# State products of a pair placed behind the outputs of the pair in front, in the unused half of their bank

## The chip, the cores and the metric

The kernel runs on one core of a Trainium2 chip. The core has TensorE (matrix products into PSUM), VectorE (DVE in the profile), ScalarE (ACT), GpSimd (POOL), SyncE (SP, which issues transfers) and 16 DMA engines. The metric is the time of one execution on the device in microseconds (us); lower is better. Numbers like L519 are lines of the kernel's source. The changed kernel has its own line numbers.

## The reference

Two blocks follow each other. The first is a state space recurrence over 4 batches of 8 heads with 768 time steps each, head size 32 and state size 16:

```python
log_a = np.log(np.clip(a, 1e-06, 1.0))
for c in range(nc):                       # chunks of 32 steps
    cum = np.cumsum(la, axis=-1)
    L = np.exp(cum[..., :, None] - cum[..., None, :]) * causal
    CB = np.einsum('bhin,bhjn->bhij', Cc, Bc)
    y_intra = np.einsum('bhij,bhjd->bhid', CB * L, xc)
    y_inter = np.einsum('bhin,bhnd->bhid', Cc, state) * np.exp(cum)[:, :, :, None]
    y[:, :, sl] = y_intra + y_inter
    Bx = np.einsum('bhjn,bhjd->bhjnd', Bc, xc) * decay_from_j[..., None, None]
    state = decay_full[:, :, None, None] * state + np.sum(Bx, axis=2)
```

Its outputs, as 3072 tokens of 256 features, go through a two-layer block with a leaky slope per hidden feature (2048 hidden features):

```python
h = x @ w_in
g = np.maximum(h, 0.0) + alpha * np.minimum(h, 0.0)
return g @ w_out
```

All is in float32.

## The kernel before

The kernel takes chunks of 128 steps and handles them in pairs: 12 pairs, 0 to 11, three to a batch. Two pairs make a group of 512 tokens; there are 6 groups. For each pair TensorE transposes B and C, multiplies them ("gram" products), adds up the outputs y, and makes the state products (B, scaled by the decays to the end of the chunk, times x). For the last pair of a batch only the first chunk's state is needed. The second block runs per group in four "quads" (z = 0 to 3), each with seven products in and seven products out: a two-by-two matrix product done with seven instead of eight products. While group g goes through its quads, the two pairs of group g + 1 are worked in between, piece by piece. Group 0 has been through the second block in another, simpler way before that.

A pair is a generator: each `next` runs it up to its next `yield`. `fine` is true for pairs 4 to 11.

```python
def pair(gp):
    ...
    tp = spare() if gp == 1 else ss_tile()
    for i in range(2):
        for k in range(2):
            nc.tensor.transpose(tp[:, (2 * i + k) * P : (2 * i + k + 1) * P], nat[:, i, k], ident)   # L469
    bc = work.tile([P, 4, Q], F32, name="bc")
    nc.scalar.copy(out=bc.rearrange("p i t -> p (i t)"), in_=tp)
    ...
    bn = bns.pop(gp) if gp in bns else pair_loads(gp)      # GpSimd: B times the decays (L385)
    ...
    def added(dps):                                        # the state products
        dps = dps.rearrange("p (k m) -> p k m", m=P)
        for k in range(nk):                                # nk = 1 for the last pair of a batch, else 2
            for w in range(KC):
                ws = slice(64 * w, 64 * w + 64)
                nc.tensor.matmul(dps[ws, k], bn[:, k, ws], xt[:, k, w * P : (w + 1) * P],     # L519
                                 start=True, stop=True, tile_position=(0, 64 * w), ...)
        return dps

    def states(dps):                                       # VectorE adds the decayed old state
        ...                                                # (ScalarE copies, for a batch's first)
        nc.gpsimd.tensor_tensor(out=sm[:, :nk], in0=new[:, :nk], in1=hmask..., op=ALU.mult)   # L534

    if fine:
        for k in range(2):
            for w in range(2):
                half_decays(k, w)                          # two scans on VectorE each (L438)
                if k == 1 and w == 1:
                    spread_c()
                yield
    ...
        if fine:
            states(added(ss_tile()))
            c_decayed()                                    # GpSimd
        yield
        gram = products_bc()
    ... # gram times decays on VectorE, with a yield in the middle and one behind
    y = [ss_tile()[:, : 2 * Q].rearrange("p (k t) -> p k t", k=2) for w in range(KC)]
    ... # 4 products with the states (L620) and 16 with dec and x (L627) into y[0] and y[1]
    for w in range(KC):
        nc.scalar.copy(out=xts[g][:, w, q * Q : (q + 2) * Q], in_=y[w]...)                    # L634
```

`ss_tile` gives a PSUM tile of 128 x 512 numbers, which is a whole bank; two banks take turns. A y fills half of its bank.

The quad, cut to its order. `first` puts two products of the first layer into half-filled tiles A or Y; `after(j)` is where products of the second layer, steps of the pairs and other work come in:

```python
first(A, b11); copy m1 <- A (ScalarE); after(1)
first(Y, t1);  copy m5 <- Y (ScalarE); after(2); after(3)
first(A, t2);  copy u2 <- A (ScalarE, L787); after(4)
Y = Y + u2 (VectorE, L789); after(5)
first(A, t3);  c22 = A + m5 (VectorE, L793); after(6)
first(Y, b22); prelu of Y and c22 (ScalarE L753, VectorE L755); copy Y <- m1 (ScalarE, L799)
after(7); after(8)
first(A, t4);  prelu of A; after(9); after(10)
first(Y, b21); prelu of Y; ... after(11) to after(14)
```

The steps of the pairs in the quads, with `nxt` the first pair of the group ahead:

```python
token_sums(1)
ssm(2 * GC // 2, 2)                 # pair 4, two steps: transposes, first scans
steps = {(0, 1): 0, (0, 2): 0, (0, 5): 0, (0, 9): 0, (0, 13): 0, (1, 1): 0, (1, 5): 0,
         (1, 12): 1, (1, 14): 1, (2, 1): 1, (2, 2): 1, (2, 5): 1, (2, 9): 1, (2, 13): 1,
         (3, 1): 1, (3, 5): 1, (3, 12): 2, (3, 14): 2}
...
def after(j, ...):
    places = with_gram if nxt < NP and z % 2 == 0 else without
    if i and j in places:
        product(*divmod(NZ + i - 1, NZ), places[j])        # second-layer products, L745
    ...
    if nxt + steps.get((z, j), NP) < NP:
        ssm(nxt + steps[z, j])
    if nxt < NP and (z, j) == (3, 7):
        token_sums(g + 1)                                  # GpSimd, L725
    ahead = nxt + {(1, 3): 1, (3, 8): 2}.get((z, j), NP)
    if ahead < NP:
        ...
        bns[ahead] = pair_loads(ahead)                     # bn of the pair ahead
```

Of the kernel before, what the change touches and what calls it, by code (L numbers as in the profile page):

```python
# [9 lines left out]
F32 = mybir.dt.float32  # L10
U32 = mybir.dt.uint32
U16 = mybir.dt.uint16
ALU = mybir.AluOpType
# [9 lines left out]
def kernel(  # L23
# [25 lines left out]
    nc = tc.nc  # L49
# [6 lines left out]
    P = 128  # L56
    Q = 128
# [6 lines left out]
    KC = d_model // P  # L64
    NF = d_ff // P
    GC = 4
    GT = GC * Q
    NG = NCH // GC
    NP = NCH // 2
# [18 lines left out]
    work = ctx.enter_context(tc.tile_pool(name="work", bufs=2))  # L88
# [4 lines left out]
    gp = ctx.enter_context(tc.tile_pool(name="gp", bufs=16))  # L93
    op = ctx.enter_context(tc.tile_pool(name="op", bufs=3))
# [172 lines left out]
    def keep_warm(to, n, cols=2 * Q):  # L267

        for i in range(n):
# [8 lines left out]
                          in_=ident.unsqueeze(1).to_broadcast([P, H, Q]))  # L278
# [11 lines left out]
    hmask = bmask[:, :P]  # L290
# [30 lines left out]
    state = {}  # L321

    masked = {}
# [2 lines left out]
    held = {}  # L326
    bns = {}

    def identity_bank():
# [47 lines left out]
    def pair_loads(gp):  # L377

        b, c = divmod(2 * gp, CPB)
        nat, abc, xt, ap = loads["p", gp]  # L380

        bn = work.tile([P, 2, H * N], F32, name="bn")
        i, bi = divmod(b, 2)
        pj = prt[i].rearrange("p (b h c) -> p b c h", b=2, h=H)[:, bi, c : c + 2]
        nc.gpsimd.tensor_tensor(  # L385
            out=bn.rearrange("p k (h n) -> p k h n", h=H),
            in0=nat[:, 0].rearrange("p k (h n) -> p k h n", h=H),
            in1=pj.unsqueeze(3).to_broadcast([P, 2, H, N]), op=ALU.mult)
        return bn
# [22 lines left out]
    def spare():  # L412

        return ps_h.tile([P, GT], F32, name="hp", tag="hp")

    def pair(gp):

        b, c = divmod(2 * gp, CPB)
        nat, abc, xt, ap = loads["p", gp]
        last = c + 2 == CPB  # L420
        dec = work.tile([P, 2, H, Q], F32, name="dec")
        dv = dec.rearrange("p k h t -> p k (h t)")

# [18 lines left out]
        ahead = {}  # L442

        pf = ap
        if gp == 0:
            z = first_a(ap, nc.vector)
# [5 lines left out]
                                    op1=ALU.min)  # L452
# [8 lines left out]
            yield  # L461


        tp = spare() if gp == 1 else ss_tile()
        if gp == 0:
            keep_warm(tp, 3, Q)
# [22 lines left out]

        fine = gp >= 2 * GC // 2  # L490
        if gp < 2:
            spread_c()
        if gp == 0:
# [1 line left out]
            dps = spare()  # L495
            keep_warm(dps, 6, Q)
            yield
        bn = bns.pop(gp) if gp in bns else pair_loads(gp)
        if gp == 1:
            c_decayed()  # L500
            dps = spare()
# [1 line left out]
        elif gp:  # L503
            yield

        nk = 1 if last else 2
        st = [masked.get(b)]  # L510
        new = work.tile([P, 2, P], F32, name="state")
        sm = work.tile([P, 2, P], F32, name="sm")

        def added(dps):
            dps = dps.rearrange("p (k m) -> p k m", m=P)
            for k in range(nk):
                for w in range(KC):
                    ws = slice(64 * w, 64 * w + 64)
                    nc.tensor.matmul(dps[ws, k], bn[:, k, ws], xt[:, k, w * P : (w + 1) * P],  # L519
                                     start=True, stop=True, tile_position=(0, 64 * w),  # L520
                                     skip_group_check=True)
            return dps

        def states(dps):
            for k in range(nk):
                old = state.get(b)
                if old is None:
                    nc.scalar.copy(out=new[:, k], in_=dps[:, k])
                else:
                    e = (k + 1) * Q - 1  # L530
                    nc.vector.scalar_tensor_tensor(out=new[:, k], in0=old, scalar=pf[:, e : e + 1],
                                                   in1=dps[:, k], op0=ALU.mult, op1=ALU.add)
                state[b] = new[:, k]
            nc.gpsimd.tensor_tensor(out=sm[:, :nk], in0=new[:, :nk],  # L534
                                    in1=hmask.unsqueeze(1).to_broadcast([P, nk, P]), op=ALU.mult)
            st.extend(sm[:, k] for k in range(nk))
            masked[b] = st[-1]

        if fine:
            for k in range(2):  # L540
                for w in range(2):
                    half_decays(k, w)
                    if k == 1 and w == 1:
                        spread_c()
                    yield
        else:
            if gp > 1:
                states(added(ss_tile()))
                c_decayed()
# [33 lines left out]
        if gp == 0:  # L583
            gram = products_bc()
            dps = added(dps)
            yield
            c_decayed()
            times(dec[:, :, :2], one_less(gram))
        elif gp == 1:
            decays(1)  # L590
            gram = products_bc()
            g0 = one_less(gram)
            states(dps)
            times(dec[:, :, :2], g0)
        else:
            if fine:
                states(added(ss_tile()))
                c_decayed()
            yield
            gram = products_bc()  # L600
        for i, r in enumerate(r for r in ((2, 3, 0, 1) if fine else (3, 2, 1, 0) if gp > 1 else range(4))
                              if r in gram):
# [6 lines left out]
        yield  # L609


        y = [ss_tile()[:, : 2 * Q].rearrange("p (k t) -> p k t", k=2) for w in range(KC)]
        if gp < 2:
            keep_warm(y[0].rearrange("p k t -> p (k t)"), 2 - gp)
        begun = False
# [359 lines left out]
    for f in range(FIRST, NF):  # L975
# [21 lines left out]
        if f in in_steps:  # L997
            weight_sums(wi, in_sums, 0, in_steps[f])
    early[0] = None
    token_sums(1)  # L1000
    ssm(2 * GC // 2, 2)


    steps = {(0, 1): 0, (0, 2): 0, (0, 5): 0, (0, 9): 0, (0, 13): 0, (1, 1): 0, (1, 5): 0,
             (1, 12): 1, (1, 14): 1, (2, 1): 1, (2, 2): 1, (2, 5): 1, (2, 9): 1, (2, 13): 1,
             (3, 1): 1, (3, 5): 1, (3, 12): 2, (3, 14): 2}

    late_sums = {(0, 2): ((wqt, out_sums, 0, 0),), (0, 4): ((wqt, out_sums, 0, 1),),
# [11 lines left out]
    for i in range(NZ * (NG - 1)):  # L1020
        g, z = divmod(NZ + i, NZ)
        nxt = 2 * g + 2

        def after(j, g=g, z=z, i=i, nxt=nxt):
            places = with_gram if nxt < NP and z % 2 == 0 else without
            if i and j in places:
                product(*divmod(NZ + i - 1, NZ), places[j])
            if i == 0:
                for f, half in last_out.get(j, ()):
                    output(NF - LATE + f, half)  # L1030
            if (i, j) in ((0, 13), (1, 8)):
# [24 lines left out]
        quad(g, z, after)  # L1056
# [31 lines left out]
```

## Time and profile before

| | before |
|---|---|
| time, median of 3 | 376.63 us (376.53 to 378.01) |
| span of the profiled execution | 375.5 us |
| TensorE busy, products | 365.0 us, 97% |
| VectorE / ScalarE / GpSimd busy | 242.4 / 179.1 / 202.1 us |
| state products L519, all pairs | 80 records, 7.0 us (5.7 into ss, 1.3 into hp) |

A busy time counts an engine's instructions, not its waits. A float32 product is recorded as two passes, each with its own weight load (PEld), so two chunks of state products, 4 instructions, appear as x8. In a line of a timeline the columns are start, length, engine, source line, operation, output <- input, shapes, how many, and in brackets how long the engine sat idle ahead of it and which instruction ended that. Runs of like instructions are merged. "issue" means that the profile shows nothing the engine waited for.

### The profile page before, as it was taken

The numbers are of one execution on the slowest core, as the hardware profiler recorded it, in microseconds if no ns is written. First come the engines' busy times: TensorE is split into PE (matmuls) and PEld (weight loads), VectorE is DVE, ScalarE is ACT, GpSimd is POOL, SyncE is SP. The second block draws the span as 40 slices with busy tenths as digits, with TensorE's granted clock in tenths as the row PEclk, the third lists the DMA queues.
The fourth block names the chain that finished last, engine by engine and source line by source line (L and its number), as shares of the span: only waits on it lengthen the run. The fifth ranks groups of instructions, "written<-read, shape, count | busy, mean of one in ns | idle before, by whom it ended". The sixth has DMA issues, their size and how long they took to land.

```text
span 375.5 us, 6180 instructions
## 1 busy us (share of the span) xinstructions
PE 365.0 (97%) x2223; PEld 294.9 (79%) x2223; DVE 242.4 (65%) x461; ACT 179.1 (48%) x384; POOL 202.1 (54%) x212
## 2 busy tenths in 40 slices
PE   8899899899999999999999999999999999999996
PEld 8676566468878788788788788788788788888884
DVE  7997959967537737747737847637847734544364
ACT  1557757425354445445445535535625525553541
POOL 4875665468856835535555445456354355264512
PEclk9999999999999999999999999999999999999999
DMA  7999898551008801002802801901811001001003
GB/s 141 222 178 290 238 234 207 146 104 58 28 19 160 159 3 56 2 0 45 165 4 47 164 2 34 178 0 23 152 38 26 5 0 20 11 0 30 1 0 84
DMA packets 121878, 30.71 MB, mean 82 GB/s; under 512 B 93736, under 2 KB 117752, under 8 KB 121848
## 3 DMA queue, kind: packets, MB, share of 16 engines
q1 hardware_dynamic: 116736, 29.74, 35.9%
q10 hardware_dynamic: 5112, 0.59, 1.1%
q8 instruction: 17, 0.28, 0.3%
q14 instruction: 13, 0.11, 0.1%
HBM read 26.98 MB, written 3.34 MB: 81 GB/s over the span
## 4 chain that ended last, share of the span: by engine, by line
PE 86%; DVE 6%; POOL 2%; ACT 2%; issue 1%; POOLq 0%; DVEq 0%; ACTq 0%
PE hp L770 33%; PE bank L745 32%; PE bank L684 4%; PE hp L646 3%; DVE dec L438 2%; PE ss L627 2%; PE hp L661 2%; PE ss L569 2%; PE ss L620 1%; PE ss L469 1%; PE ss L519 1%; PE hp L569 1%; PE hp L270 1%; DVE gt L650 1%; DVE wr L239 1%
## 5 line engine op out<-in xcount | busy, mean ns | idle before, releaser
L813 POOL TENSOR_TENSOR gt<-gt 128x512 f32<-128x512 f32 x58 | 73.6, 1269 | 31.4 <-DVE gt L755 24.5
L755 DVE SCALAR_TENSOR_TENSOR gt<-hp,s_mul,gt 128x256 f32<-128x256 f32 x120 | 52.5, 479 | 47.7 <-ACT gt L753 46.4
L745 PE MATMUL bank<-gt,w_out 128*128 128x256 f32 x320 | 82.5, 382 | 0.4 <-ACT o_sb L691 0.4
L753 ACT ACTIVATE gt<-hp,s_alpha 128x256 f32<-128x256 f32 x120 | 50.3, 470 | 46.8 <-PE hp L770 32.7
L745 PEld LDWEIGHTS bank<-gt,w_out 128*128 128x128 f32 x320 | 60.0, 190 | 11.2 <-issue 2.3
L804 POOL TENSOR_TENSOR gt<-gt 128x512 f32<-128x512 f32 x20 | 25.4, 1270 | 77.7 <-DVE gt L755 77.7
L745 PE MATMUL bank<-gt,ws 128*128 128x256 f32 x240 | 58.3, 379 | 0.0
L745 PEld LDWEIGHTS bank<-gt,ws 128*128 128x128 f32 x240 | 45.1, 190 | 5.8
L438 DVE TENSOR_TENSOR_SCAN dec<-abc,bank 128x256 f32<-128x256 f32 x80 | 48.1, 661 | 0.0
L770 PE MATMUL hp<-xs,w_in 128*128 128x256 f32 x160 | 42.8, 390 | 0.0
L770 PE MATMUL hp<-xT,w_in 128*128 128x256 f32 x160 | 41.9, 384 | 0.0
L770 PE MATMUL hp<-xs,ws 128*128 128x256 f32 x160 | 41.1, 379 | 0.0
L789 DVE TENSOR_TENSOR hp<-hp,u 128x512 f32<-128x512 f32 x20 | 14.0, 700 | 39.6 <-ACT u L787 39.6
L778 ACT COPY m<-hp 128x512 f32<-128x512 f32 x20 | 11.7, 586 | 51.5 <-PE hp L770 51.5
L770 PEld LDWEIGHTS hp<-xs,w_in 128*128 128x128 f32 x160 | 28.7, 189 | 7.7 <-issue 3.3
L770 PEld LDWEIGHTS hp<-xT,w_in 128*128 128x128 f32 x160 | 29.7, 190 | 5.1 <-issue 1.2
L770 PEld LDWEIGHTS hp<-xs,ws 128*128 128x128 f32 x160 | 30.4, 190 | 4.1
L684 PEld LDWEIGHTS bank<-w_out,gt 128*128 128x128 f32 x128 | 24.2, 190 | 8.7 <-issue 5.8
L684 PE MATMUL bank<-w_out,gt 128*128 128x256 f32 x128 | 30.5, 380 | 0.0
L646 PE MATMUL hp<-xT,w_in 128*128 128x512 f32 x48 | 23.2, 605 | 3.4 <-DVE gt L650 2.6
L793 DVE TENSOR_TENSOR c<-hp,m 128x512 f32<-128x512 f32 x20 | 13.6, 681 | 19.3 <-PE hp L770 19.3
L787 ACT COPY u<-hp 128x512 f32<-128x512 f32 x20 | 11.7, 585 | 23.0 <-PE hp L770 23.0
(155 smaller groups left out, 554.0 us busy)
## 6 DMA issues: line engine op xcount, KB each, us to landing
abc<-z SPq DMA_DIRECT2D x20, 512.0 KB, 4.8
raw<-in_moe_w_in_dram SPq DMA_DIRECT2D x8, 512.0 KB, 4.9
raw<-in_moe_w_out_dram SPq DMA_DIRECT2D x8, 512.0 KB, 6.3
xt<-in_x_dram SPq DMA_DIRECT2D x24, 128.0 KB, 3.9
out_dram<-o_sb SPq DMA_DIRECT2D x32, 64.0 KB, 1.9
nat<-in_B_dram SPq DMA_DIRECT2D x22, 64.0 KB, 2.6
nat<-in_C_dram SPq DMA_DIRECT2D x22, 64.0 KB, 2.6
ap<-pf SPq DMA_DIRECT2D x11, 128.0 KB
```

What stands on the lines that cost most here:

```text
L438: nc.vector.tensor_tensor_scan(out=dv[:, k, hs], data0=abc[k][:, hs], data1=ident_p[0], initial=0.0, op0=ALU.mult, op1=ALU.add)
L646: nc.tensor.matmul(hp, w_in[:, k, f * P : (f + 1) * P], xts[g][:, k], start=(k == 0), stop=(k == KC - 1))
L684: nc.tensor.matmul(pos[0][t // 2][:, t % 2], gt[:, t * Q : (t + 1) * Q], w_out[:, f], start=(f == 0 and t % 2 == 0), stop=(f == NF - 1), s ...
L745: nc.tensor.matmul(ms[g][i][:, h], w, blocks[g, z][n][:, p], start=(q == 0 and h == 0), stop=(q == NQ - 1), skip_group_check=True)
L753: nc.scalar.mul(o[:, p], h[:, p], s_alpha[:, fs[p]])
L755: nc.vector.scalar_tensor_tensor(out=o[:, p], in0=h[:, p], scalar=s_mul[:, fs[p]], in1=o[:, p], op0=ALU.mult, op1=ALU.max)
L770: nc.tensor.matmul(to[:, p], w(2 * z + p), b, start=start and p == 0, stop=True, skip_group_check=True)
L778: nc.scalar.copy(out=m1, in_=A)
L789: nc.vector.tensor_tensor(out=Y, in0=Y, in1=u2, op=ALU.add)
L793: nc.vector.tensor_tensor(out=c22, in0=A, in1=m5, op=ALU.add)
L804: nc.gpsimd.tensor_tensor(out=tc_, in0=g22, in1=g12, op=ALU.subtract)
L813: eng.tensor_tensor(out=o, in0=x0, in1=x1, op=ALU.subtract)
```

## The change

The state products of a pair leave their own step in the even quads, (0, 9) and (2, 9). They come at (1, 5) and (3, 5), straight behind the outputs of the pair in front, and go into the second half of the bank that holds that pair's y[1]. That takes one PSUM tile per pair out of the rotation. On TensorE the products with small tiles (the outputs, 32 columns wide, and the state products, 64 wide) then stand side by side, and the stream of full products in the even quads is no longer broken at (z, 9). For this bn must be ready sooner, so GpSimd makes it at (0, 9) and (2, 9) instead of (1, 3) and (3, 8). `c_decayed` moves to the last scan. Pair 4, which has no fine pair in front, gets a tile of its own, and its state products become its first step, ahead of its transposes.

```diff
@@ pair
+        if fine:
+            bn = bns.pop(gp) if gp in bns else pair_loads(gp)
+            states(added(beside.pop(gp) if gp in beside else ss_tile()[:, : 2 * Q]))
+            yield
+
         tp = spare() if gp == 1 else ss_tile()
         ... (transposes, bc, spread_c and c_decayed as before)
-        bn = bns.pop(gp) if gp in bns else pair_loads(gp)
+        if not fine:
+            bn = bns.pop(gp) if gp in bns else pair_loads(gp)
         ...
         if fine:
             for k in range(2):
                 for w in range(2):
                     half_decays(k, w)
                     if k == 1 and w == 1:
                         spread_c()
+                        c_decayed()
                     yield
         ...
-            if fine:
-                states(added(ss_tile()))
-                c_decayed()
-            yield
+            if not fine:
+                yield
             gram = products_bc()
         ...
-        y = [ss_tile()[:, : 2 * Q].rearrange("p (k t) -> p k t", k=2) for w in range(KC)]
+        ys = [ss_tile() for w in range(KC)]
+        y = [t[:, : 2 * Q].rearrange("p (k t) -> p k t", k=2) for t in ys]
+        if fine:
+            beside[gp + 1] = ys[1][:, 2 * Q :]
@@ the loop over the quads
-    ssm(2 * GC // 2, 2)
+    ssm(2 * GC // 2, 3)
-    steps = {..., (0, 9): 0, ..., (2, 9): 1, ...}
+    steps = {...}                      # the same without (0, 9) and (2, 9)
             if nxt + steps.get((z, j), NP) < NP:
                 ssm(nxt + steps[z, j])
+            if j == 5 and z % 2 and nxt + z // 2 + 1 < NP:
+                ssm(nxt + z // 2 + 1)
-            ahead = nxt + {(1, 3): 1, (3, 8): 2}.get((z, j), NP)
+            ahead = nxt + {(0, 9): 1, (2, 9): 2}.get((z, j), NP)
```

More of the change, by code (lines that the diff above doesn't have):

```diff
@@ L327 @@
     bns = {}
+    beside = {}
     def identity_bank():
@@ L420, in pair @@
         last = c + 2 == CPB
+        fine = gp >= 2 * GC // 2
         dec = work.tile([P, 2, H, Q], F32, name="dec")
@@ L461, in pair, with added, states @@
             yield
+        nk = 1 if last else 2
+        st = [masked.get(b)]
+        new = work.tile([P, 2, P], F32, name="state")
+        sm = work.tile([P, 2, P], F32, name="sm")
+        def added(dps):
+            dps = dps[:, : 2 * Q].rearrange("p (k m) -> p k m", m=P)
+            for k in range(nk):
+                for w in range(KC):
+                    ws = slice(64 * w, 64 * w + 64)
+                    nc.tensor.matmul(dps[ws, k], bn[:, k, ws], xt[:, k, w * P : (w + 1) * P],
+                                     start=True, stop=True, tile_position=(0, 64 * w),
+                                     skip_group_check=True)
+            return dps
+        def states(dps):
+            for k in range(nk):
+                old = state.get(b)
+                if old is None:
+                    nc.scalar.copy(out=new[:, k], in_=dps[:, k])
+                else:
+                    e = (k + 1) * Q - 1
+                    nc.vector.scalar_tensor_tensor(out=new[:, k], in0=old, scalar=pf[:, e : e + 1],
+                                                   in1=dps[:, k], op0=ALU.mult, op1=ALU.add)
+                state[b] = new[:, k]
+            nc.gpsimd.tensor_tensor(out=sm[:, :nk], in0=new[:, :nk],
+                                    in1=hmask.unsqueeze(1).to_broadcast([P, nk, P]), op=ALU.mult)
+            st.extend(sm[:, k] for k in range(nk))
+            masked[b] = st[-1]
+        if fine:
+            bn = bns.pop(gp) if gp in bns else pair_loads(gp)
+            states(added(beside.pop(gp) if gp in beside else ss_tile()[:, : 2 * Q]))
+            yield
         tp = spare() if gp == 1 else ss_tile()
@@ L488, in c_decayed @@
                                     op=ALU.mult)
-        fine = gp >= 2 * GC // 2
         if gp < 2:
@@ L504, in pair @@
             yield
[L509 to L537, printed above, removed]
         if fine:
@@ L1000 @@
     token_sums(1)
-    ssm(2 * GC // 2, 2)
-    steps = {(0, 1): 0, (0, 2): 0, (0, 5): 0, (0, 9): 0, (0, 13): 0, (1, 1): 0, (1, 5): 0,
-             (1, 12): 1, (1, 14): 1, (2, 1): 1, (2, 2): 1, (2, 5): 1, (2, 9): 1, (2, 13): 1,
+    ssm(2 * GC // 2, 3)
+    steps = {(0, 1): 0, (0, 2): 0, (0, 5): 0, (0, 13): 0, (1, 1): 0, (1, 5): 0,
+             (1, 12): 1, (1, 14): 1, (2, 1): 1, (2, 2): 1, (2, 5): 1, (2, 13): 1,
              (3, 1): 1, (3, 5): 1, (3, 12): 2, (3, 14): 2}
```

## Prediction

> **What bounds the kernel now.** I read the page first, then busy time by stretch, then the waits, then the timelines of TensorE's weight loads and of the engines that feed it. Page, busy shares:
>
> ```profile
> PE 365.0 (97%) x2223; PEld 294.9 (79%) x2223; DVE 242.4 (65%) x461; ACT 179.1 (48%) x384; POOL 202.1 (54%) x212
> ```
>
> Busy time of each engine by stretch (columns: stretch, its length, then PE, PEld, DVE, ACT, POOL, clock, DMA share, GB/s):
>
> ```profile
> 113.00:127.40 14.40, 14.40 (x73) 11.82 (x72) 11.26 (x21) 7.77 (x17) 11.01 (x10) 1.00 0.89 157
> 141.50:312.00 170.50, 170.48 (x1057) 141.65 (x1056) 109.88 (x219) 80.22 (x179) 84.08 (x83) 1.00 0.26 52
> ```
>
> TensorE never idles in the stages that the change touches (84 to 312 us); the others have a quarter of their time or more free. So time put into TensorE's stream there, a wait too, lengthens the kernel one for one, unless the stream would have waited at the same place anyway. The waits give the size of what little waiting there is:
>
> ```profile
> PEld hp L770 <- ACT u L787: 1.3, 6, 0.2
> ```
>
> The weight load behind such a copy starts 0.05 or 0.11 us after the copy's end (119.62 after 119.50, for one). I use that as the hand-over from ScalarE to TensorE.
>
> What the state products cost where they stand (TensorE's weight loads; pair 5 with one chunk, then pair 4 with two):
>
> ```profile
> 122.96 0.84 PEld L770 LDWEIGHTS hp<-xs,w_in 128*128 128x128 f32 x4
> 124.13 0.20 PEld L519 LDWEIGHTS ss<-xt,bn 128*64 128x64 f32 x4 [0.33 <-issue]
> 124.50 0.73 PEld L770 LDWEIGHTS hp<-xT,w_in 128*128 128x128 f32 x4 [0.17 <-issue]
> 125.25 0.84 PEld L745 LDWEIGHTS bank<-gt,w_out 128*128 128x128 f32 x4
> ```
>
> ```profile
> 92.50 0.84 PEld L770 LDWEIGHTS hp<-xs,w_in 128*128 128x128 f32 x4
> 93.67 0.42 PEld L519 LDWEIGHTS ss<-xt,bn 128*64 128x64 f32 x8 [0.33 <-issue]
> 94.26 0.73 PEld L770 LDWEIGHTS hp<-xT,w_in 128*128 128x128 f32 x4 [0.17 <-issue]
> ```
>
> A group of four full loads repeats every 0.865 (a later one: 125.25 to 126.12). Without L519 the L745 group would start at 122.96 + 2 x 0.865 = 124.69; it starts at 125.25. A one-chunk group costs 0.56. With two chunks the next L684 group starts at 95.01, so it costs 95.01 - 92.50 - 1.73 = 0.78. Most of that is the gap of 0.33 ahead and 0.17 behind, the change of the array's tile shape.
>
> **What the Trainium skill says.** "TensorEngine Tiling (Array Packing)", Key Properties: changing the tiling mode drains TensorE. The trace agrees: 0.33 us idle ahead of each L519 group, and between the 64x128 products L620 and the 128x32 products L627 there is a gap too (loads 191.57 to 192.09, then from 192.22). The new neighbours have 128x32 and 128x64 tiles, two modes, so I do not expect the drain to vanish between them. "PSUM — Partial Sum Buffer", PSUM bank collisions raise a hardware error: two engines may not touch one bank in the same partitions at once, even at other addresses, so waits go by bank and not by address. This decides the case. The built order of the changed kernel agrees: its state products wait for the ScalarE copy of y[1], whose bank they share, although they write the other half. The trace before cannot show it, since there they have a bank of their own. "TensorE: Matmul & The Clock Gate", What's actually happening: after an idle window of about 3.4 us the array runs at half rate. The trace shows clock 1.00 throughout, with no gap in TensorE's loads over 2.2 us.
>
> **Part 1, taken out of the even quads (z = 0 and 2, j = 9).** Eight groups go: pairs 4, 6, 7, 9, 10 with two chunks, 5, 8, 11 with one: 5 x 0.78 + 3 x 0.56 = 5.6 us. Not all comes back, because the b21 product behind them waits for ScalarE to put m1 into Y:
>
> ```profile
> 123.48 0.59 ACT L799 COPY hp<-m 128x512 f32<-128x512 f32 x1 [0.20 <-DVE gt L755]
> ```
>
> It ends at 124.07. Without L519, b21 would be ready at 122.96 + 0.865 = 123.82 and wait until 124.12 to 124.18. After a pause four loads take 0.75 (124.50 to 125.25), so the next group starts at 124.87 to 124.93, against 124.69: 0.18 to 0.24 of waiting takes the group's place. The same sum with each even quad's own copy gives 2.4 to 2.9 us over eight (the longest, 0.65, near 210 us, where the combination of the group before also loads ScalarE). Part 1 is worth 5.6 - 2.6 = 3.0 us.
>
> **Part 2, put behind the outputs of the pair in front (z = 1 and 3, j = 5).** Weight loads, then ScalarE, around one such place:
>
> ```profile
> 192.22 0.81 PEld L627 LDWEIGHTS ss<-dec,xt 128*32 128x32 f32 x32
> 193.23 0.73 PEld L770 LDWEIGHTS hp<-xs,w_in 128*128 128x128 f32 x4 [0.20 <-issue]
> ```
>
> ```profile
> 193.15 0.65 ACT L634 COPY xT<-ss 128x256 f32<-128x256 f32 x2 [1.75 <-PE ss L627]
> ```
>
> The two copies of y end at 193.80. The state products stand ahead of L770 in TensorE's queue and wait for the second copy: start 193.85 to 193.91. From their first load to the next full load it is 0.59 with two chunks (93.67 to 94.26) and 0.37 with one (124.13 to 124.50). So L770 starts near 194.47 instead of 193.23: 1.24 more; 1.02 with one chunk. At all eight places the copies end 0.88 us after the last L627 load has started. Seven pairs go this way (5 to 11): 4 x 1.24 + 3 x 1.02 = 8.0 us. Nothing hides it: all else in TensorE's queue stands behind.
>
> VectorE's state update (0.34 each) then runs while t3's product does, ahead of c22, which waits for that product anyway: no cost. GpSimd's mask of the state (0.73) comes ahead of the token sums at (3,7); these end near 199, and the next group needs them after 202. No cost.
>
> **Part 3, pair 4.** It has no fine pair in front, so its products get a bank of their own, and now stand ahead of its transposes L469, at the end of the first phase. They need bn. GpSimd, then the weight loads:
>
> ```profile
> 84.51 0.73 POOL L725 TENSOR_TENSOR xs<-xT 128x256 f32<-128x256 f32 x1
> ...
> 86.69 0.73 POOL L725 TENSOR_TENSOR xs<-xT,xs 128x256 f32<-128x256 f32 x1
> 87.38 0.64 POOL L385 TENSOR_TENSOR bn<-nat,prt 128x256 f32<-128x256 f32 x1
> ```
>
> ```profile
> 82.56 1.49 PEld L684 LDWEIGHTS bank<-w_out,gt 128*128 128x128 f32 x7 [0.24 <-issue]
> 84.07 0.58 PEld L469 LDWEIGHTS ss<-ident,nat 128*128 128x128 f32 x4
> ```
>
> GpSimd works without a pause from 82.06 to here, in an order that the change leaves alone up to bn. So bn ends at 88.02. The products start at 88.07, and L469 at 88.07 + 0.59 = 88.66 instead of 84.07: 4.5 us, less the 0.1 that a stream gets back after a pause. VectorE's two state updates wait too and hold the six scans (3.57) behind them; those then end near 93.1, and the next step on VectorE's path, the sum into Y (L789, at 89.07 before), comes 4.5 later, at 93.6. They just fit.
>
> **Sum.** 376.6 + 4.5 + 8.0 - 3.0 = 386.1 us.
>
> **Rivals.** (a) The wish behind the change: no wait counts, and a mode change is saved. Then Part 2 costs at most 4 x 0.59 + 3 x 0.37 = 3.5 and, if 128x32 to 128x64 needs no drain, 0.2 less each, about 2.1; with Part 1 at -3.0 and Part 3 nil: 375.7 to 377.1. For it speaks only that the data are ready; against it, the wait on the bank in the program. (b) Part 2 as above but bn done early enough: 381.6, still the same within 2%. Against it is GpSimd's unbroken row of work up to bn. (c) TensorE idles 3.8 us at 84 to 88 and its clock falls: some 3.4 us at half rate, 1.7 or more lost, 388 to 389. The window must lie wholly in the gap, which is barely longer; I give it one in seven. (d) The delay is taken up later, because TensorE would have waited anyway: the stretches leave room only for the 1.3 us of u2 waits and one wait of 1 us near 111 us, and both hang on TensorE's own earlier products, so they move along.
>
> **Range and chances.** Parts 1 and 2 may be off by 0.5 and 1.0; Part 3 is one place and firm, if GpSimd reaches it on time; the clock adds to the top. Range 383.3 to 389.0. The 2% line is 384.2, 1.9 below my value: to get there, Part 3 must be half as big or Part 2 a quarter smaller. Slower by over 2%: 0.78; same: 0.20; faster: 0.02, since nothing removed adds up to 7.5 us.
>
> **What would show it.** In the changed profile: a gap of about 4 us in the weight loads ahead of the state products near 84 us, released by GpSimd's bn; seven gaps of 0.9 between the outputs and the state products, released by the ScalarE copy of xT; in each even quad a pause of 0.3 ahead of b21 behind the m copy; clock 1.00. I am wrong if the state products follow the outputs within 0.4, if bn comes before 85, or if an idle TensorE turns up elsewhere.

## The result and the profile after

| | before | after |
|---|---|---|
| time, median of 4 runs | 376.99 us (376.53 to 378.01) | 388.55 us (387.75 to 389.77) |
| ratio after / before, 95% interval | | 1.0306 [1.0269, 1.0343] |
| span of the profiled execution | 375.5 us | 387.9 us |
| TensorE busy, products | 365.0 us | 368.4 us |
| VectorE / ScalarE / GpSimd busy | 242.4 / 179.1 / 202.1 us | 244.3 / 179.2 / 202.0 us |

The change costs 11.6 us. Each engine executes as many instructions as before, so the time went into waits and into a slower clock. Lines moved in the changed kernel: the state products are L478 (before L519), the transposes L509 (L469), the y products L629 and L636 (L620, L627), the xT copies L643 (L634), the first layer of the quad L779 (L770), its second layer L754 (L745), the copy of m1 into Y L808 (L799), the first phase's outputs L693 (L684).

Three views of the profile after show it. First the page: busy times, and the granted clock in 40 slices, each digit a tenth of full speed.

```profile
PE 368.4 (95%) x2223; PEld 295.9 (76%) x2223; DVE 244.3 (63%) x461; ACT 179.2 (46%) x384; POOL 202.0 (52%) x212
...
PEclk9999899998999999999999999999999999999999
```

TensorE is still the bound. Two slices at 8, near 45 and near 90 us, are new: before, every slice stood at 9. Then the waits of the weight loads (who waited for what: us in total, how often, the longest):

```profile
PEld ss L478 <- issue: 6.5, 9, 0.8
PEld ss L478 <- POOL bn L387: 4.0, 1, 4.0
PEld hp L779 <- ACT hp L808: 2.9, 8, 0.4
PEld hp L779 <- ACT u L796: 1.6, 7, 0.3
```

The first three are the three parts of the prediction: the state products behind the outputs (seven of the nine waits of that line, 5.8 us; two of 0.33 lie in the first phase), pair 4's wait for bn, and the waits for m1 that appear in the even quads. The first is put down to "issue", that is, to nothing that this view shows; experiments 2, 4 and 6 find its cause. Third, the stretches (stretch, length, then busy time of PE, PEld, DVE, ACT, POOL, the clock, DMA share and GB/s):

```profile
84.00:90.10 6.10, 2.55 (x10) 1.52 (x8) 0.77 (x2) 0.69 (x1) 5.85 (x7) 1.00 0.00 0
90.30:93.70 3.40, 3.40 (x16) 2.73 (x15) 2.45 (x6) 0.58 (x1) 1.61 (x2) 0.50 0.00 0
93.70:103.00 9.30, 9.30 (x43) 7.71 (x42) 6.13 (x12) 5.66 (x13) 5.88 (x6) 1.00 0.19 58
146.00:320.00 174.00, 170.93 (x1041) 141.86 (x1043) 111.89 (x219) 81.02 (x179) 84.14 (x83) 1.00 0.26 51
```

TensorE idles while only GpSimd works; then comes a stretch at half rate, which ends as sharply as it began. And from 146 to 320 us TensorE now idles 3.07 us in all, where before 170.48 of 170.50 us were busy.

The places themselves. Pair 4 (weight loads, then GpSimd; start, length, engine, line, operation, in brackets the idle time ahead and what ended it):

```profile
84.66 1.49 PEld L693 LDWEIGHTS bank<-w_out,gt 128*128 128x128 f32 x7 [0.24 <-issue]
90.14 0.63 PEld L478 LDWEIGHTS ss<-xt,bn 128*64 128x64 f32 x8 [4.00 <-POOL bn L387]
91.10 0.71 PEld L509 LDWEIGHTS ss<-ident,nat 128*128 128x128 f32 x4 [0.33 <-issue]
```

```profile
88.77 0.72 POOL L734 TENSOR_TENSOR xs<-xT,xs 128x256 f32<-128x256 f32 x1
89.45 0.64 POOL L387 TENSOR_TENSOR bn<-nat,prt 128x256 f32<-128x256 f32 x1
```

bn follows the last token sum without a pause and ends at 90.09, as the prediction read it from before; the load starts 0.05 later. (In the profiled execution all of this lies 2.1 us later than in the profile before; that came earlier, in the first phase, and is taken up below.) One of the places behind the outputs, weight loads and then ScalarE:

```profile
172.18 0.81 PEld L636 LDWEIGHTS ss<-dec,xt 128*32 128x32 f32 x32
173.83 0.45 PEld L478 LDWEIGHTS ss<-xt,bn 128*64 128x64 f32 x8 [0.83 <-issue]
174.44 0.73 PEld L779 LDWEIGHTS hp<-xs,w_in 128*128 128x128 f32 x4 [0.17 <-issue]
```

```profile
173.11 0.65 ACT L643 COPY xT<-ss 128x256 f32<-128x256 f32 x2 [1.52 <-PE ss L636]
```

The two copies of y end at 173.76, and 0.07 later the state products start. From the start of the last L636 load to the first L478 load it is 0.944 us, at all seven places alike. The waiting itself stands in the trace as an instruction of TensorE's sequencer (PEldq: count, then shortest, median and longest in ns):

```profile
L478 PEldq EVENT_SEMAPHORE  x12: 51/1356/1357, 11.6 to 290.4; - x12
```

Each of the seven ahead of these groups waits for a semaphore that ScalarE raises, besides that of a transfer; the one here starts at 172.45 and ends at 173.80. So the wait is one that the built program holds. An even quad, where the state products went away:

```profile
190.40 0.84 PEld L779 LDWEIGHTS hp<-xs,w_in 128*128 128x128 f32 x4
191.61 0.73 PEld L779 LDWEIGHTS hp<-xT,w_in 128*128 128x128 f32 x4 [0.38 <-ACT hp L808]
192.37 0.62 PEld L754 LDWEIGHTS bank<-gt,w_out 128*128 128x128 f32 x3
```

Undisturbed, two groups of 0.865 would lead from 190.40 to 192.13; L754 starts at 192.37. The wait for m1 thus eats 0.24 us of what the removal brings.

### The profile page after: what moved, and what is told of

Same layout as the page of the kernel before. It is cut to its first block, busy times and chain, and to the rows that moved or that the text cites. A ratio compares the mean times of both kernels' runs of the same rounds, so it can differ in the third digit from the quotient of the medians.

```text
span 387.9 us, 6165 instructions
## 1 busy us (share of the span) xinstructions
PE 368.4 (95%) x2223; PEld 295.9 (76%) x2223; DVE 244.3 (63%) x461; ACT 179.2 (46%) x384; POOL 202.0 (52%) x212
## 4 chain that ended last, share of the span: by engine, by line
PE 81%; DVE 7%; POOL 3%; issue 3%; DMA 2%; ACT 2%; ACTq 0%; POOLq 0%; SPq 0%; DVEq 0%
PE hp L779 32%; PE bank L754 31%; PE bank L693 3%; PE hp L655 3%; DVE dec L441 2%; PE ss L636 2%; PE hp L670 2%; PE ss L577 2%; PE ss L629 1%; PE ss L478 1%; PE ss L509 1%; DMA nat<-in_C_dram 1%; DVE gt L659 1%; DMA nat<-in_B_dram 1%; PE hp L577 1%
## 5 line engine op out<-in xcount | busy, mean ns | idle before, releaser
L754 PE MATMUL bank<-gt,w_out 128*128 128x256 f32 x320 | 82.5, 382 | 0.4 <-ACT o_sb L700 0.4
L754 PEld LDWEIGHTS bank<-gt,w_out 128*128 128x128 f32 x320 | 60.0, 190 | 11.2 <-issue 2.3
L754 PE MATMUL bank<-gt,ws 128*128 128x256 f32 x240 | 58.3, 379 | 0.0
L754 PEld LDWEIGHTS bank<-gt,ws 128*128 128x128 f32 x240 | 45.1, 190 | 5.8
L779 PE MATMUL hp<-xs,w_in 128*128 128x256 f32 x160 | 42.9, 390 | 0.0
L779 PE MATMUL hp<-xT,w_in 128*128 128x256 f32 x160 | 42.7, 390 | 0.1
L779 PE MATMUL hp<-xs,ws 128*128 128x256 f32 x160 | 41.1, 379 | 0.0
L779 PEld LDWEIGHTS hp<-xT,w_in 128*128 128x128 f32 x160 | 30.2, 193 | 6.7 <-ACT hp L808 2.9
L779 PEld LDWEIGHTS hp<-xs,w_in 128*128 128x128 f32 x160 | 28.7, 189 | 7.5 <-issue 2.8
L779 PEld LDWEIGHTS hp<-xs,ws 128*128 128x128 f32 x160 | 30.5, 191 | 4.3
L693 PEld LDWEIGHTS bank<-w_out,gt 128*128 128x128 f32 x128 | 24.6, 193 | 9.3 <-issue 6.6
L693 PE MATMUL bank<-w_out,gt 128*128 128x256 f32 x128 | 30.8, 382 | 0.0
L655 PE MATMUL hp<-xT,w_in 128*128 128x512 f32 x48 | 24.7, 639 | 3.4 <-DVE gt L659 2.7
L493 POOL TENSOR_TENSOR sm<-state,bmask 128x256 f32<-128x256 f32 (+1 forms) x12 | 7.6, 636 | 38.7 <-DVE state L490 36.6
```

The costliest lines, as they stand in the source:

```text
L655: nc.tensor.matmul(hp, w_in[:, k, f * P : (f + 1) * P], xts[g][:, k], start=(k == 0), stop=(k == KC - 1))
L693: nc.tensor.matmul(pos[0][t // 2][:, t % 2], gt[:, t * Q : (t + 1) * Q], w_out[:, f], start=(f == 0 and t % 2 == 0), stop=(f == NF - 1), s ...
L754: nc.tensor.matmul(ms[g][i][:, h], w, blocks[g, z][n][:, p], start=(q == 0 and h == 0), stop=(q == NQ - 1), skip_group_check=True)
L779: nc.tensor.matmul(to[:, p], w(2 * z + p), b, start=start and p == 0, stop=True, skip_group_check=True)
```

## The experiments

The theory: Part 2 is the wait for the second ScalarE copy, because the state products share its bank; Part 3 is bn's place in GpSimd's queue; both add up, and behind the long gap of Part 3 TensorE's clock falls. The rivals: the state products are slow where they stand because of the change of tile shape itself; or one wait hides in the other, so that undoing one brings nothing.

| run | what it is | us, median (range, runs) | ratio to before |
|---|---|---|---|
| 1 e1_bn_early | after, bn of pair 4 earlier | 382.89 (382.04 to 383.72, 4) | 1.0148 [1.0131, 1.0165] |
| 2 e2_ahead_of_copy | after, state products ahead of the copies | 383.27 (381.34 to 384.43, 4) | 1.0161 [1.0127, 1.0194] |
| 3 e3_both | 1 and 2 | 377.88 (377.67 to 379.14, 10) | 1.0023 [1.0013, 1.0032] |
| 4 e8_first_bank | 1, in the bank of y[0] | 380.34 (380.18 to 381.57, 4) | 1.0094 [1.0081, 1.0107] |
| 5 e4_warm | after, the gap filled with 9 idle products | 386.84 (386.02 to 387.86, 4) | 1.0262 [1.0240, 1.0284] |
| e9_warm_two | after, 2 idle products | 387.73 (386.74 to 388.73, 4) | 1.0284 [1.0251, 1.0316] |
| 6 e5_tile32 | 3, state products in four tiles of 32 columns | 376.57 (376.32 to 378.19, 13) | 0.9992 [0.9983, 1.0001] |
| 7 e6_tile32_half | 6, and half a product moved | 375.65 (375.16 to 377.23, 8) | 0.9967 [0.9955, 0.9979] |
| e7_before_half | before, half a product moved | 377.12 (376.61 to 378.47, 13) | 1.0003 [0.9994, 1.0012] |

The kernel before took 377.12 us beside runs 1, 2, 3 and 5, 377.01 beside 4, 6, 7 and e7, and 377.05 beside e9.

**1. bn of pair 4 made earlier.** GpSimd makes it in the first phase, ahead of the token sums. Nothing else changes.

```diff
@@ first phase, step f
+        if f == 13:
+            bns[4] = pair_loads(4)
```

> The changed kernel (388.5 us), with bn of pair 4 made on GpSimd some ten microseconds sooner, in the first phase, instead of behind the token sums. Theory (pair 4's products wait 4 us for bn, and the idle stretch then costs TensorE half its clock for 3.4 us): the gap ahead of pair 4's state products falls from 4.0 us to the 0.33 of a mode change, the half-rate stretch behind it goes, and the time falls by 5 to 5.5 us, to about 383.3. Rival (the clock falls for other reasons, or the time is lost in the quads): the gap goes but the time falls by less than 3 us, to 386 or more.

Measured: 382.89 us, 5.7 less than the changed kernel. TensorE's weight loads at pair 4:

```profile
83.76 1.49 PEld L693 LDWEIGHTS bank<-w_out,gt 128*128 128x128 f32 x7 [0.24 <-issue]
85.58 0.42 PEld L478 LDWEIGHTS ss<-xt,bn 128*64 128x64 f32 x8 [0.33 <-issue]
86.16 0.42 PEld L509 LDWEIGHTS ss<-ident,nat 128*128 128x128 f32 x4 [0.17 <-issue]
```

The gap of 4.00 has shrunk to the 0.33 of a change of tile shape, and the clock stays at full rate through 80 to 100 us. So the gap was the wait for bn, and it was paid in full: GpSimd did the same work in another order, and nothing took the gap's place.

**2. The state products ahead of the copies.** The pair behind is advanced right after the y products are emitted, so its state products come ahead of the two ScalarE copies in the program, and the copies wait for them instead of the other way round. They stay in the same half of the same bank.

```diff
@@ pair
-            states(added(beside.pop(gp) if gp in beside else ss_tile()[:, : 2 * Q]))
+            dps = added(beside.pop(gp) if gp in beside else ss_tile()[:, : 2 * Q])
+            yield
+            states(dps)
             yield
 ...
+        if fine and gp + 1 < NP:
+            ssm(gp + 1)
         for w in range(KC):
             nc.scalar.copy(out=xts[g][:, w, q * Q : (q + 2) * Q], ...)
@@ ahead of the quads
-    ssm(2 * GC // 2, 3)
+    ssm(2 * GC // 2, 4)
```

> The changed kernel (388.5 us), with the state products put between the output products and the ScalarE copies of y in program order, so that they no longer wait for a copy; the copy of y[1] waits for them instead. Pair 4 as in the changed kernel. Theory (the wait for the bank costs 0.64 us at each of seven places): 0.94 us from the last output load to the first state load becomes 0.31, and the time falls by 4.5 us, to about 384.1. Rival (the later copy of y[1], 0.6 us, holds up VectorE's c22 and the prelu chain, or the products for the bank are slow beside the copy): the time falls by less than 2.5 us. If the modes 128x32 and 128x64 need no drain between them, the distance becomes 0.11 and the time falls by 5.8 us.

Measured: 383.27 us, 5.3 less than the changed kernel. From the last y load to the first state load it is now 0.308 us at all places instead of 0.944. The waits of L478, to be held against the first fence of waits above:

```profile
PEld ss L478 <- POOL bn L387: 4.0, 1, 4.0
...
PEld ss L478 <- issue: 2.1, 9, 0.3
```

"issue" fell from 6.5 to 2.1 and its longest from 0.8 to 0.3, while the instructions and their neighbours on TensorE stayed. The semaphore instructions at the seven places no longer name ScalarE, and each lasts 51 ns instead of 1356. So 4.4 of the 6.5 us were the wait for the copy. The wait for bn, which this edit leaves alone, stayed at 4.0.

**3. Both.**

> Both repairs at once: bn of pair 4 sooner, and the state products ahead of the copies. Theory (two causes that add up, each on TensorE's path): 378 to 379 us, the sum of both gains, and still 1 to 2 us over the kernel before, since the group behind the outputs costs 0.62 (two chunks) or 0.40 (one) there and leaves a wait for the copy of m1 in the even quads. Rival (the intended saving is real once the waits are gone): below 376 us.

Measured: 377.88 us, 10.7 less than the changed kernel; the two alone brought 5.7 and 5.3. They add up within 0.3, so neither hides behind the other. One place behind the outputs (weight loads):

```profile
163.26 0.81 PEld L638 LDWEIGHTS ss<-dec,xt 128*32 128x32 f32 x32
164.27 0.42 PEld L478 LDWEIGHTS ss<-xt,bn 128*64 128x64 f32 x8 [0.20 <-issue]
164.86 0.73 PEld L783 LDWEIGHTS hp<-xs,w_in 128*128 128x128 f32 x4 [0.17 <-issue]
```

What is left is 0.20 idle ahead and 0.17 behind. The idea without its two waits is only 0.2% from the kernel before.

**4. In the bank of y[0].** Run 1 with one index changed: the state products take the free half of the bank whose copy comes first. They stand in the same place with the same neighbours, and must only wait for one copy instead of two. If bank sharing makes the wait, it gets shorter by what lies between the ends of the two copies; if the half or the tile shape made it, nothing changes.

```diff
-            beside[gp + 1] = ys[1][:, 2 * Q :]
+            beside[gp + 1] = ys[0][:, 2 * Q :]
```

> The changed kernel with bn of pair 4 sooner (382.9 us), and the state products in the second half of y[0]'s bank instead of y[1]'s, so that they wait for the first of the two copies, which ends 0.27 us sooner. Theory (the wait goes by the bank's copy): 0.67 instead of 0.94 us at each of seven places, 1.9 us less, 381.0. Rival (the wait is for something else that takes as long, such as the state products' inputs or a drain): no change.

Measured: 380.34 us, 2.5 less than run 1, and the distance is 0.668 us instead of 0.944. From the first state load of pair 4 to the last load of the kernel it is 375.94 - 85.45 = 290.49 us, against 378.02 - 85.58 = 292.44 in run 1: 1.95 less, which is seven times 0.276. The rest of the 2.5 lies outside this stretch. Weight loads:

```profile
165.37 0.81 PEld L636 LDWEIGHTS ss<-dec,xt 128*32 128x32 f32 x32
166.74 0.45 PEld L478 LDWEIGHTS ss<-xt,bn 128*64 128x64 f32 x8 [0.56 <-issue]
```

Idle ahead of the state products: 0.83 behind two copies, 0.56 behind one, 0.20 behind none. The wait follows the copy of the bank, although no copy touches the half that is written. In every run a bank is also one tile of the program, so whether the program's wait is set by the bank or by the tile is not separated.

**5. The gap filled, so that only the clock differs.** Products with unused values, written into pair 4's own tile ahead of its state products, keep TensorE busy while it waits for bn. The wait stays; a fall of the clock should not come. Its sister e9 does the same with 2 products instead of 9; what both add is overwritten.

```diff
-            states(added(beside.pop(gp) if gp in beside else ss_tile()[:, : 2 * Q]))
+            to = beside.pop(gp) if gp in beside else ss_tile()[:, : 2 * Q]
+            if gp == 4:
+                keep_warm(to, 9)         # e9_warm_two: 2
+            states(added(to))
```

> The changed kernel (388.5 us), with nine products of ones into pair 4's own tile ahead of its state products, which fill TensorE's 4 us gap; their values are overwritten. Theory (the clock falls because TensorE idles there): no half-rate stretch behind the gap, L779's first loads 0.22 apart instead of 0.43, and 1.3 to 1.7 us less, about 387.0. Rival (the clock falls by chance or for another reason): half rate stays near 90 to 94 us and the time stays at 388 to 389.

Measured: 386.84 us. Weight loads at pair 4, and the stretch behind:

```profile
83.53 3.86 PEld L270 LDWEIGHTS ss<-warm 128*128 128x128 f32 x18
87.72 0.42 PEld L478 LDWEIGHTS ss<-xt,bn 128*64 128x64 f32 x8 [0.33 <-POOL bn L387]
88.31 0.42 PEld L512 LDWEIGHTS ss<-ident,nat 128*128 128x128 f32 x4 [0.17 <-issue]
```

```profile
90.00:94.00 4.00, 4.00 (x20) 3.30 (x19) 3.49 (x7) 2.43 (x5) 3.92 (x5) 1.00 0.36 109
```

The clock stays full: no gap, no half rate. L512 comes 88.31 - 83.53 = 4.78 us after the end of the first phase's stream, where before L469 followed directly. Of this about 0.2 is the filler's own: GpSimd's bn ended at 87.47, and the state products started not 0.05 later but at 87.72, behind the last idle product and a change of tile shape. In the profiled executions the way from the first state load of pair 4 to the last weight load of the kernel is 380.11 - 87.72 = 292.39 us here and 384.15 - 90.14 = 294.01 in the changed kernel: the stretch at half rate costs 1.6 us. The medians differ by 388.55 - 386.84 = 1.7, though 0.2 of run 5 is the filler.

A further run on the clock left part of the gap open:

> The changed kernel (388.5 us), with only two products of ones at the start of TensorE's gap ahead of pair 4's state products: 0.9 us of it is filled, some 3.1 us stay idle. The Trainium skill (TensorE: Matmul & The Clock Gate) says that the clock falls after an idle window of about 3.4 us, which no longer fits in. Theory: no half-rate stretch behind the gap, 386.8 as with nine products, since the wait for bn is the same. Rival (any long wait of TensorE there makes the clock fall): half rate at 90 to 94 us again, 388.5.

Measured: 387.73 us, inconclusive. The profiled execution shows the load behind a gap of 3.13 us, and full rate behind it:

```profile
84.67 0.84 PEld L270 LDWEIGHTS ss<-warm 128*128 128x128 f32 x4
88.64 0.42 PEld L478 LDWEIGHTS ss<-xt,bn 128*64 128x64 f32 x8 [3.13 <-POOL bn L387]
```

But this execution was the fastest of the four (386.74 us, mean clock 0.999). The others took 387.53 to 388.73 at 0.991 to 0.995, so they had a half-rate stretch somewhere, and where is not recorded. The length of the gap alone does not settle it; where the gap lies matters too (see "The clock" below).

**6. The same tile shape as the neighbour.** What is left between outputs and state products in run 3 is the change from 32 to 64 columns. Here the state products are split into four of 32 columns, as the outputs have, twice as many instructions for the same numbers.

```diff
-                for w in range(KC):
-                    ws = slice(64 * w, 64 * w + 64)
+                for r in range(4):
+                    ws, w = slice(32 * r, 32 * r + 32), r // 2
                     nc.tensor.matmul(dps[ws, k], bn[:, k, ws], xt[:, k, w * P : (w + 1) * P],
-                                     start=True, stop=True, tile_position=(0, 64 * w), ...)
+                                     start=True, stop=True, tile_position=(0, 32 * r), ...)
```

> Both repairs (377.9 us), with the state products split into tiles of 32 columns instead of 64, so that they run in the mode of the output products in front of them. Theory (every change of mode drains the array, 128x32 to 128x64 too): the distance from the last output load to the first state load falls from 0.31 to 0.11 us at seven places, and the time by 1.4, to 376.5, some 0.6 below the kernel before. Rival (the distance is the small tiles' own pipeline, or twice as many instructions cost as much): no change, 377.9.

Measured: 376.57 us, 1.3 less than run 3. Weight loads:

```profile
163.27 0.81 PEld L638 LDWEIGHTS ss<-dec,xt 128*32 128x32 f32 x32
164.06 0.46 PEld L478 LDWEIGHTS ss<-xt,bn 128*32 128x32 f32 x16
164.71 0.73 PEld L783 LDWEIGHTS hp<-xs,w_in 128*128 128x128 f32 x4 [0.20 <-ACT xT L647]
```

The distance falls from 0.308 to 0.089 us, so 0.22 was the change of shape. The group itself is 0.06 longer up to L783 (0.65 against 0.59). That leaves 0.16 at each of seven places, 1.1 us: from the first state load of pair 4 to the last load it is 371.13 - 84.44 = 286.69 us, against 371.90 - 84.11 = 287.79 in run 3. With this the saving that the change aimed at is there, and it only just repays the rest: the interval of the ratio touches 1.

**7. The wait for m1 filled, and its control.** In the even quads the b21 product waits for m1 now that the state products no longer cover it. Half of a second-layer product is moved from the place (2, 3) to (2, 9).

```diff
 def product(g, z, n, ps=(0, 1)):
-        for p in range(2):
+        for p in ps:
@@ after(j)
-                product(..., places[j])
+                parted = places is with_gram and z == 2 and j == 3
+                product(..., places[j], (0,) if parted else (0, 1))
+            if i and places is with_gram and z == 2 and j == 9:
+                product(..., places[3], (1,))
```

> As the one with tiles of 32 columns, and in quads z = 2 half of the product placed at j = 3 moves to j = 9, where TensorE waits for the copy of m1 since the state products left. Theory (the wait left in the even quads is 0.35 and 0.25 of it is lost): 0.2 us less in each of four quads, less what the shorter filling at j = 3 costs, so 0.4 to 0.8 less than with tiles of 32 alone, near 376.0. Rival (the stretch from j = 3 to j = 5 then waits as much for ScalarE's copies): no change.

> The kernel before, with only the half product moved in quads z = 2. Theory: there the state products already fill the wait at j = 9, so nothing is won, 377.0 to 377.5. Rival: if it wins 0.5 or more, the gain of the run with both is not due to the place of the state products.

Measured: 375.65 us with it, and for the same move in the kernel before 377.12, no difference. Weight loads of run 7 around the place:

```profile
179.39 0.84 PEld L783 LDWEIGHTS hp<-xs,w_in 128*128 128x128 f32 x4
180.25 0.41 PEld L758 LDWEIGHTS bank<-gt,w_out 128*128 128x128 f32 x2
180.68 0.84 PEld L783 LDWEIGHTS hp<-xT,w_in 128*128 128x128 f32 x4
```

The loads follow each other without a pause, and the waits for m1 fell from 2.9 us at eight places to

```profile
PEld hp L783 <- ACT hp L812: 1.3, 4, 0.3
```

So filling the wait that Part 1 leaves was worth about 0.9 us (376.57 - 375.65). The waits are gone at the four places of z = 2, and three of those at z = 0 fell from 0.43 to 0.33. In the kernel before, the same move has next to nothing to fill: only one place waits for m1 there, 0.26 us at 210.87. This version beats both kernels, by 0.33% [0.21%, 0.45%] against the kernel before.

## Why the prediction was right

The prediction said 386.1 us, 383.3 to 389.0; measured were 388.55. All three parts came at the places and with the causes it named. Its value was 2.5 too low: the fall of the clock behind the gap, a rival to which it gave one in seven, adds 1.6, a second such fall in half of the executions about 0.7, the kernel before came out 0.4 above the 376.6 taken for it, and 0.5 cannot be placed; against these, the three parts together cost 0.8 less than predicted. That errors of opposite sign offset each other here is luck.

**Part 1** (-3.0 predicted) was worth more. The waits for m1 came in every even quad, 0.24 us at 190 us for instance, and 0.19 at pair 5 (1.92 - 1.73), for which 0.18 to 0.24 had been worked out. From the end of the first phase's stream on, Parts 1 and 2 together can be read without the clock: from the transposes of pair 4 to the last load it is 371.77 - 84.07 = 287.70 us before and 378.02 - 86.16 = 291.86 in run 1, so +4.2. With Part 2 at 8.1 this leaves -3.9 for Part 1. The single places add up to the same. Removed are 5.7: the group near 210 cost 0.65 and not 0.56, because b21 waited for m1 even there. The waits that remain in run 1, each counted like the 0.24 above, are 2.0 in all. And a small transpose (L368 at 138.97 before, 0.21 up to the next load), which is made together with the bn of pair 6, moved with it and now fits into the wait at pair 5 (L370 in run 1): 0.2 more, which the prediction left out. The mis-sized term is the 2.6 taken for the waits; the largest, predicted as 0.65 near 210 us, was 0.3, since the copy of m1 there ended 1.22 us after the start of the group ahead and not 1.57 as in the kernel before.

**Part 2** (+8.0) held. The distance of 0.944 is the 0.88 read from the copies of the kernel before plus the hand-over of 0.07. Per place it costs 1.253 with two chunks and 1.035 with one, 4 x 1.253 + 3 x 1.035 = 8.1. This part rested on the Trainium skill, "PSUM — Partial Sum Buffer", PSUM bank collisions raise a hardware error: two engines may not be at one bank in the same partitions at once. The runs agree so far that the program makes the writer of one half wait for the reader of the other (run 4); what the chip does without that wait, no run shows. Rival (a), that no wait counts, needed the state products to follow within 0.4 us; they do only once they are issued ahead of the copies (run 3), and then the time is 377.88, 0.8 above the 375.7 to 377.1 that (a) gave. Its second half, no change of shape between 128x32 and 128x64, fell: the Trainium skill, "TensorEngine Tiling (Array Packing)", Key Properties, has each change of mode drain TensorE, and run 6 puts 0.22 us on it for just these two shapes.

**Part 3** (+4.5) held. In the changed kernel the stream of the first phase gives way at 86.17, and L478 starts at 90.14: 3.97 us, against 88.07 - 84.07 = 4.00 predicted. L509 follows 0.96 later, at half rate; at full rate it is 0.59, as predicted and as in run 5. Rival (b), bn early enough, is run 1, and did not happen by itself: GpSimd's row up to bn was as unbroken as it looked. VectorE's order held too: two states, then six scans, 3.57 us from 91.86.

**The clock**, rival (c), is the step that failed: "The window must lie wholly in the gap", and with it the one in seven. TensorE's products idled from 86.55 to 90.15, 3.60 us, and at 90.28 the clock fell to 0.50 until 93.69. That costs the 1.6 us of run 5. The Trainium skill, "TensorE: Matmul & The Clock Gate", What's actually happening, names an idle window of about 3.4 us. The profiles show that less idling is enough. In each of them the granted clock changes only on a grid of steps of 3.413 us that runs on through the execution: in the changed kernel it is full for 40.96 us ahead of each of the falls at 45.91 and 90.28, 12 steps, and in the kernel before for 368.64 us on end, 108 steps. The step ahead of each fall (stretch, length, then busy time of PE and the rest as above):

```profile
42.50:45.91 3.41, 1.76 (x19) 1.02 (x18) 3.35 (x7) 1.84 (x4) 1.88 (x2) 1.00 0.84 103
86.87:90.28 3.41, 0.13 (x2) 0.14 (x4) 0.00 (x0) 0.00 (x0) 3.14 (x5) 1.00 0.00 0
```

TensorE was busy 1.76 and 0.13 us there. The other falls inside the work followed steps with 1.77 and 0.05 us (run 2), 1.64 (run 1) and 1.67 (run 4); no step with 1.78 us or more was followed by one. A step with 1.75 in e9 was not either, so the limit, near half a step, is not sharp to 0.03 us in these records. By these figures a gap of 3.60 us leaves too little work in some step wherever the grid cuts it: cut in the middle, each of the two steps keeps about 1.6 us (an estimate, 3.41 less half of 3.60). The gap of 3.13 us in e9 was cut at 87.33, both steps kept 2.00 us or more, and no fall came.

The executions that were not profiled fit. The mean clock of the four was 0.990, 0.996, 0.991 and 0.996, and one stretch of 3.41 us at half rate lowers the mean of 386 us by 0.0044, so every one of them had at least one such stretch. One thing does not fit and stays open: run 2 has the same gap, and one of its four executions, not profiled, shows 1.000.

**The sum.** Part 3 at 4.5 and Parts 1 and 2 at 4.2 make 8.7. The profiled execution of e9, which has the changed kernel's wait at pair 4 (3.97 us from stream to L478) and full clock, agrees: its last load comes at 381.02 against 371.77 before, 9.25 later, of which 84.67 - 84.07 = 0.60 was there before the first state product. The prediction had 4.5 + 8.0 - 3.0 = 9.5, 0.8 more, all of it Part 1. Without the clock this is 377.0 + 8.7 = 385.7 us; with the stretch behind the gap, 1.6, it is 387.3.

The two executions of the changed kernel at 0.996 took 387.75 and 388.16; the two at 0.990 and 0.991, with room for a second stretch, 389.77 and 388.94. In the profiled one the second stretch lies in the first phase, at 45.9 to 49.3 us, which the change does not touch; the cost of such a one can be read between runs 1 and 3, which differ up to pair 4 by little more than a stretch of that kind at 14 us: 85.58 - 84.11 = 1.5 us. Half of that in the median gives 388.05. The 0.5 up to 388.55 is of the size by which the first phase differs from one profiled execution to another (its end at 84.07 before, 84.67 in e9, 83.53 in run 5); I cannot split it further. Where the stretches of the executions that were not profiled lie is inferred from their mean clock, not seen. Rival (d), a delay taken up later, fell: from the first state load of pair 4 to the last load it is 378.02 - 85.58 = 292.44 us in run 1 and 371.90 - 84.11 = 287.79 in run 3, and the difference of 4.65 is all of seven times the 0.64 by which the waits differ, and a little more.

## What to carry to other kernels

An unused half of a PSUM bank was not free space beside a reader: the program makes a product put there wait for whoever reads the other half. Issuing it before the reader removed that wait; a bank of its own at the same place, as the kernel before had it elsewhere, was not tried. When an operation is moved forward to fill a gap, follow what it needs back through the other engines' queues; one input that stands behind a row of unrelated work there stops the whole stream of the engine that bounds the kernel, and here a stop of 3.6 us cost 1.6 us more in clock. Moving work away from a place also uncovers what it was covering: plan a filler for that wait with the move, since only the version with all of these beat the kernel before.

## What the runs showed of the hardware that was not expected

- The half-rate stretches inside the profiled executions each last 3.41 us. The one at 90.28 us began 0.13 us after the gap had ended, so the price falls on the work behind the gap and not into it.
- Such stretches also came in the first phase, where TensorE's products had idled only 1.65 us at a time (43.92 to 45.57, then half rate from 45.91). The profile of the kernel before has the same pause (1.62 us, 43.55 to 45.18) and no fall: there the grid cuts it at 44.64, and the two steps are busy 2.33 and 2.87 us. So the same stream can fall or not fall with where the grid happens to lie.
- A change between 128x32 and 128x64 tiles costs 0.22 us (0.308 against 0.089 between the loads); between full products and small tiles the loads idle 0.33 us ahead and 0.17 behind.
- A wait for a ScalarE copy can stand in the waits as "issue" when a semaphore instruction of its own ahead of the loads does the waiting: 4.4 of the 6.5 us were the copy, as the same line of run 2 shows.
